# An order table in place of a list scheduler, in an attention and FFN kernel on one Trainium2 core

## The chip, the cores and the metric

The kernel runs on one core of a Trainium2 chip. The metric is the device time of one execution in microseconds; the program has one launch. The core has five engines with queues of their own: TensorE (PE in the profile; PEld is its weight load), VectorE (DVE), ScalarE (ACT), GpSimd (POOL) and SyncE (SP). Sixteen DMA engines move data for all of them.

## The reference

Windowed attention with sinks, then a gated feed-forward layer on its output, in float32:

```python
B, H, S, D = 4, 8, 768, 64;  n_sink, window = 4, 128
scores = q @ k.T / sqrt(D)                # per batch and head
keep = (key < n_sink) | (0 <= query - key < window)
a = softmax(where(keep, scores, -1e9))
x = (a @ v).transpose(0, 2, 1, 3).reshape(B * S, H * D)      # 3072 x 512
xn = x / sqrt(mean(x * x) + 1e-6) * rms_g
g = xn @ w_gate                           # 512 x 1536
out = (g * sigmoid(g) * (xn @ w_val)) @ w_out                # 1536 x 512
```

## The kernel before

**Blocks and groups.** The 3072 tokens are 24 blocks of 128, six for each of the four batches. Four blocks make a group of the feed-forward layer, six groups in all. A block g goes through these steps:

- q, k and v of the block are loaded. q and k of block 0 come through SP as float32 and are cast (`load_f32`, `cast`, L326 to L331). All others are loaded by POOL's software DMA, which casts to bf16 on the way (`load_bf16` L335, `load_v` L339). The gate and value weights come in tiles `w-a-b` (columns a to b of 12, `sw_w`, L381), the output weights in two tiles (`sw_wo`, L387).
- q and k are transposed: by TensorE and a copy for blocks 0 to 7 (`pe_t` L428, `copy_t` L435), by a DMA on SP's queue from block 8 on (`dma_t`, L442).
- Scores (`scores` L468, `scores_last` L484 for the last block of a batch), exp on ScalarE (L516, L492), masks. For blocks 0 and 1 a TensorE product adds the mask ahead of the scores (`mask_bias`, L450); up to block 15 VectorE multiplies by a mask (L533, L499); from 16 on POOL does it (L538, L505). From the third block of a batch on, four sink keys take part (`sink_k`, `sink_v`, `sink_s`, `sink_e`; L644 to L680).
- The attention product with v (`av`, L552 to L569), the division by the sum (`normal`, L580 and L581, tile x), the square on ScalarE (L589), the rms chain and the scaled xr on VectorE (`rms`, L596 to L613).
- xr is transposed into xnt, by TensorE and a copy for blocks 0 to 7 (`pe_x` L628, `copy_x` L634), by a DMA on SP's queue from block 8 on (`dma_x`, L640).

A group then takes chunks of the gate and value products, each into one PSUM bank (`mms`, L863, tiles g and v; in the profile v is also the name of the attention's v). A chunk is 4 weight columns by one block for group 0 (matmuls of 128 columns), 2 by two blocks for groups 1 and 2 (256), 1 by four blocks after that (512). Tanh is on ScalarE (L870), the two products that make hT are on VectorE (p L876, hT L886). The output product (L896, in three parts of four matmuls per block), its evacuation (L904) and the store by SP (L908) follow. The last block's output is cut into halves (L914 to L932).

**What sets the order.** The kernel does not issue instructions directly. Each step is an operation that is given to `Plan.op` with its engines and durations (`ways`), the tokens that it needs and gives, a priority, and the PSUM banks that it takes and drops. `Plan.run` (L70) then works through all of them as a list scheduler: among the operations whose needs are given it picks, again and again, the one that its own clock lets start first, by priority among equals. DMA landings are estimated by `Plan.land` (L50). The functions are called in that order, and each engine runs its instructions in it. So the order is fixed when the program is built; on the chip an engine waits only for data and buffers. The needs that stand for timing alone (such as `("s", g - LOAD_LEAD)` in `sw_block`, or `sw` n-8) are the planner's; on the chip POOL's load n waits for the landing of load n-8, as its DMA waits in the trace show.

The software loads' order is a string, in which `qkv-2` stands for three loads:

```python
LOADS = "q-1 k-1 v-0 w-0-2 v-1 qkv-2 qkv-3 w-2-4 w-4-6 w-6-8 w-8-9 w-9-10 w-10-12 qkv-4 wo-0-6 qkv-5 wo-6-12 qkv-6 qkv-8 qkv-7"
LOADS += "".join(f" qkv-{g}" for g in range(9, NB))
```

`WARM` = 30 products of zeros (L403) fill TensorE's waits at the start. The float32 product `unit_gb` (L411) spreads rms_g over the partitions.

Of the kernel before, what the change touches and what calls it, by code (L numbers as in the profile page):

```python
# [10 lines left out]
ACT = mybir.ActivationFunctionType  # L11
FP32 = mybir.dt.float32
BF16 = mybir.dt.bfloat16
I32 = mybir.dt.int32

P = 128
# [8 lines left out]


class Plan:

# [4 lines left out]
    LATE = 300  # L33
    RESERVE = 8
    HOP = {"PE": 40, "ACT": 35, "DVE": 35, "POOL": 90, "SP": 60}
# [7 lines left out]
    def op(self, ways, needs=(), gives=(), prio=0.0, takes=(), drops=(), ring=None, work=0.0,  # L43
           mode=0):
        self.ops.append(dict(
            ways=ways, needs=set(needs), gives=tuple(gives), prio=prio, takes=tuple(takes),
            drops=tuple(drops), ring=ring, work=work, mode=mode, at=len(self.ops), ready=0,
        ))
# [20 lines left out]

    def run(self):  # L70
        free, users = dict(self.START), {}
        self.loads = sum(o["ring"] == "POOL" for o in self.ops)
        wait = {o["at"]: set(o["needs"]) for o in self.ops}
        cand = {e: [] for e in free}
        left = len(self.ops)
        for o in self.ops:
            for t in o["needs"]:
                users.setdefault(t, []).append(o)
            if not o["needs"]:
                for e in o["ways"]:  # L80
                    cand[e].append(o)
        busy, warm, mode, order = [], False, 0, []
        while left:
            first = None

            many = min(
                (o for o in cand["PE"] if len(o["takes"]) > self.RESERVE), default=None,
                key=lambda o: o["prio"],
            )
            for e, found in cand.items():  # L90
                for o in found:
                    k = len(o["takes"])
                    if k > len(self.banks):
                        continue
                    ready = o["ready"] + self.HOP[e] if o["ready"] else 0
                    if k:
                        ready = max(ready, sorted(self.banks.values())[k - 1] + 40)
                    start = max(free[e], ready)
                    if (k and many and o["prio"] > many["prio"] and start > many["ready"]
                            and len(self.banks) - k < len(many["takes"])):  # L100
                        continue
                    key = (start, o["prio"], ready, o["at"])
                    if first is None or key < first[0]:
                        first = key, e, o
            if first is None:
                raise RuntimeError("stuck: %s" % [
                    (o["gives"], list(wait[o["at"]])) for o in self.ops if o["at"] in wait
                ][:20])
            (start, *_), e, o = first
            for x in o["ways"]:  # L110
                cand[x].remove(o)
            wait.pop(o["at"])
            left -= 1
            ns, lat, fn = o["ways"][e]
            if e == "PE":
                busy = [(a, d) for a, d in busy if a > start - 3413]
                warm = start - free[e] < 4000 and (warm or sum(d for a, d in busy) > 3000)
                ns = ns if warm else 2 * ns
                if o["mode"] != mode:
                    ns, mode = ns + 110, o["mode"]  # L120
                busy.append((start, ns if mode != 2 else 0))
                lat = ns + 180
            for s in o["takes"]:
                i = min(self.banks, key=lambda i: (self.banks[i], i))
                del self.banks[i]
                self.held[s] = i
            free[e] = start + ns
            end = start + lat
            if o["ring"] is not None:
                end = self.land(o["ring"], end, o["work"]) + self.LATE  # L130
            for s in o["drops"]:
                self.banks[self.held[s]] = end + 12
            for t in o["gives"]:
                for x in users.pop(t, ()):
                    x["ready"] = max(x["ready"], end + 12)
                    w = wait[x["at"]]
                    w.discard(t)
                    if not w:
                        for way in x["ways"]:
                            cand[way].append(x)  # L140
            order.append((start, end, e, fn, o))
        return order


@with_exitstack
def kernel(
# [13 lines left out]
    nc = tc.nc  # L160
# [15 lines left out]
    VW = D + 1  # L176
# [7 lines left out]
    POOL_AT = (1,2)  # L184
    DEPTH = 8
    LOADS = "q-1 k-1 v-0 w-0-2 v-1 qkv-2 qkv-3 w-2-4 w-4-6 w-6-8 w-8-9 w-9-10 w-10-12 qkv-4 wo-0-6 qkv-5 wo-6-12 qkv-6 qkv-8 qkv-7"
# [75 lines left out]
    dve(70, lambda: nc.vector.memset(ident, 0.0), gives=["id0"], prio=-99)  # L262
    dve(130, lambda: nc.vector.memset(bias.bitcast(I32), 0), gives=["bias0"], prio=-98)
    for b in range(B):
        dve(60, lambda b=b: nc.vector.memset(V16[b][:, :, :, D:VW], 1.0),
            gives=[("vone", b)], prio=-97 + b if b == 0 else -50)
# [47 lines left out]
    dve(130, other_bias, [("bias", 0)], [("bias", 1)], -60)  # L314
    dve(220, cut_ident, ["ident"], ["idnos"], -59)
    dve(700, make_masks, [("bias", 0), ("bias", 1)], ["masks"], MASKS_PRIO)
    dve(300, make_sel, ["ident"], ["sel", "headm"], MASKS_PRIO + 1)

# [41 lines left out]
    def sw_load(fn, gives, work, ns=870, needs=()):  # L360
        n = len(issue)
        more = [("sw", n - DEPTH)] if n >= DEPTH else []
        op({"POOL": (ns, 1900, fn)}, list(needs) + more, list(gives) + [("sw", n)], -89 + n,
           ring="POOL", work=work)
        issue.append(n)
# [35 lines left out]
    def warm(i):  # L401
        ps = bank(("warm",)) if i == 0 else BANK[("warm",)]
        nc.tensor.matmul(out=ps[:, 0:P], lhsT=zeros, rhs=zeros, start=True, stop=True)  # L403

    for i in range(WARM):
        pe(55, lambda i=i: warm(i), ["zeros"] + ([("warm", i - 1)] if i else []),
           [("warm", i)], 1e9, takes=[("warm",)] if i == 0 else (),
           drops=[("warm",)] if i == WARM - 1 else ())

# [5 lines left out]

    pe(1000, unit_gb, ["ones", "grow"], ["gbm"], GB_PRIO, takes=[("gb",)], mode=2)
    act(490, scale_gb, ["gbm", "table"], ["gb"], drops=[("gb",)])
# [157 lines left out]
    def normal(g, u):  # L575
        if u == 0:
            T["x16", g] = xpool.tile([P, H, D], BF16, name="x16")
        pvv = BANK.pop(("av", g, u))[:, 0:HW].rearrange("p (h c) -> p h c", c=VW)
        rden = small.tile([P, 4], FP32, name="rden")
        nc.vector.reciprocal(out=rden, in_=pvv[:, :, D])  # L580
        nc.vector.tensor_tensor(  # L581
            out=T["x16", g][:, 4 * u:4 * u + 4, :], in0=pvv[:, :, 0:D],
            in1=rden.unsqueeze(2).to_broadcast((P, 4, D)), op=ALU.mult,
        )
# [119 lines left out]
    def block_scores(g):  # L704
# [10 lines left out]
        for n0, n1 in parts:  # L715
            needs = [("kT", g)] + [("qT", g + i) for i in range(n0, n1)] + gate_of(g)
            needs += [("mb", g)] if g < PE_MASKS else []
            last = (n0, n1) == parts[-1]
# [19 lines left out]
            for u in range(2):  # L738
                for hi in range(2):
                    act(215 * (n1 - n0) + 55,  # L740
                        lambda g=g, u=u, hi=hi, n=(n0, n1), last=last: exps(g, u, hi, *n, last),
                        [("s", g, n0), "table"] + ([("av", g - 2, u)] if g >= 2 else [])
                        + ([("x", g, u, 0, n0)] if hi else []),
                        [("x", g, u, hi, n) for n in range(n0, n1)], early,
                        drops=[("s", g, u, hi)] if last else ())
# [16 lines left out]
    for g in range(NB):  # L762
# [21 lines left out]
        if t + 1 == NT:  # L784
            slots = [("s", g, hi) for hi in range(2)]
            needs = [("kT", g), ("qT", g)] + gate_of(g)
            if b in MERGE:
# [150 lines left out]
    def ffn(G, n, fts, cols, prio):  # L938
# [3 lines left out]
        keys.append(key)  # L942
        pe(864, lambda: mms(bank(("g", key)), wg, G, fts, cols),
           xs + [("wg", ft) for ft in fts], [("g", key)], prio, takes=[("g", key)])
        pe(864, lambda: mms(bank(("v", key)), wv, G, fts, cols),
           [("g", key)] + [("wv", ft) for ft in fts], [("u", key), ("F", G, n)], prio - 0.5,
# [39 lines left out]

    order = plan.run()
    with tc.manual_schedule():
# [36 lines left out]
```

## Time and profile before

| | |
|---|---|
| runs | 245.15, 245.25, 245.61 us; median 245.25 |
| profiled execution | span 243.9 us from the first instruction's start to the last one's end; the rest of a run's time lies around it |
| TensorE | busy 235.3 us (96%), 2116 matmuls |
| VectorE | busy 181.1 us (74%) |
| ScalarE | busy 131.2 us (54%) |
| POOL | busy 89.5 us (37%), 86 loads among it |
| DMA | 27.35 MB; the software queue moved 13.90 MB, SP's and ACT's 12.99 MB |

A row of the profile names engine, line, operation and tiles (output<-inputs). A row of TensorE with `x16` is sixteen matmuls in a row; the span of one includes its pipeline, so the distance of starts tells what one costs. Under "DMA to landing" stands the time from the issue of a DMA to the semaphore that tells of its landing. A wait in brackets names what came last. Positions of software loads are counted in POOL's order.

### The profile page before, as it was taken

The page shows a single profiled execution, that of the slowest core. Times are in us where ns is not written, and L with a number is a line of the kernel's source. Part 1 is how long each engine was busy: PE and PEld are TensorE (multiplying, and loading weights), DVE is VectorE, ACT ScalarE, POOL GpSimd, SP SyncE. Part 2 cuts the span into 40 slices and gives each one's busy share as a digit, 9 for nine tenths or more (in the row PEclk, how much of TensorE's full clock was granted, in tenths as well). Part 3 has the DMA queues.
Part 4 walks back from the last instruction along what each step waited for, and adds up shares of the span by engine and source line. Part 5 has one row for each costly group of instructions (what it writes and reads, how often), then busy time and mean ns, then how long its engine had stood idle before and what let it go on. Part 6 is the DMA issues. An engine that isn't in the chain of part 4 may idle for free.

```text
span 243.9 us, 5513 instructions
## 1 busy us (share of the span) xinstructions
PE 235.3 (96%) x2116; PEld 148.4 (61%) x2116; DVE 181.1 (74%) x481; ACT 131.2 (54%) x268; POOL 89.5 (37%) x116
## 2 busy tenths in 40 slices
PE   4988999999999999999999999999999999999994
PEld 2558987884788875587786544544554444444443
DVE  4279979896999999999899789896379760377700
ACT  4686565769684827584844574572553311333111
POOL 8976785596435546344520130321320000000000
PEclk9999999999999999999999999999999999999999
DMA  9999999999999999999999461110231002200022
GB/s 127 151 167 196 186 187 187 159 133 163 141 194 162 155 154 156 162 225 137 128 131 143 110 171 25 22 22 21 91 108 24 1 0 86 86 3 0 0 86 86
DMA packets 113579, 27.35 MB, mean 112 GB/s; under 512 B 103697, under 2 KB 110609, under 8 KB 113554
## 3 DMA queue, kind: packets, MB, share of 16 engines
q0 software_dynamic: 81760, 13.90, 80.6%
q1 hardware_dynamic: 31650, 12.99, 28.6%
q8 instruction: 16, 0.26, 0.4%
q10 hardware_dynamic: 144, 0.13, 0.2%
q14 instruction: 9, 0.07, 0.1%
HBM read 28.31 MB, written 6.29 MB: 142 GB/s over the span
## 4 chain that ended last, share of the span: by engine, by line
PE 76%; DMA 15%; DVE 4%; POOL 2%; issue 1%; POOLq 0%
PE v L863 23%; PE g L863 22%; PE o L896 20%; DMA wv<-in_moe_w_val_dram 7%; DMA q<-in_q_dram 5%; PE s L468 3%; DMA v<-in_v_dram 3%; PE av L569 2%; PE av L562 1%; PE av L552 1%; PE o_last L914 1%; DVE e L533 1%; DVE x L581 1%; POOL wg L381 1%; POOL wv L381 1%
## 5 line engine op out<-in xcount | busy, mean ns | idle before, releaser
L863 PE MATMUL v<-xnt,wv 128*128 128x128 bf16 (+2 forms) x528 | 71.1, 282 | 0.0
L863 PE MATMUL g<-xnt,wg 128*128 128x128 bf16 (+2 forms) x528 | 69.8, 282 | 0.3 <-DMA wg<-in_moe_w_gate_dram 0.2
L870 ACT ACTIVATE th<-g 128x512 bf16<-128x512 f32 x72 | 43.2, 600 | 50.0 <-PE g L863 47.4
L896 PE MATMUL o<-wo,hT 128*128 128x512 bf16 x276 | 65.4, 379 | 0.0
L876 DVE SCALAR_TENSOR_TENSOR p<-th,g 128x512 bf16<-128x512 bf16 x72 | 47.9, 682 | 21.6 <-ACT th L870 21.4
L863 PEld LDWEIGHTS <-wg 128*128 128x128 bf16 x528 | 43.1, 98 | 19.7 <-DMA wg<-in_moe_w_gate_dram 0.6
L863 PEld LDWEIGHTS <-wv 128*128 128x128 bf16 x528 | 43.1, 98 | 19.2 <-issue 0.5
L886 DVE TENSOR_TENSOR hT<-p,v 128x512 bf16<-128x512 bf16 x72 | 47.1, 680 | 1.5 <-PE v L863 0.7
L516 ACT ACTIVATE e<-s 128x512 bf16<-128x512 f32 (+1 forms) x88 | 43.8, 569 | 7.2 <-PE s L468 5.8
L896 PEld LDWEIGHTS <-hT 128*128 128x128 bf16 x276 | 25.3, 98 | 26.5 <-issue 1.5
L904 ACT ACTIVATE osb<-o 128x512 f32<-128x512 f32 x23 | 13.8, 601 | 23.4 <-PE o L896 23.4
L335 POOL DMA_DIRECT2D k<-in_k_dram x23 | 20.4, 886 | 16.3 <-DMA v<-in_v_dram 11.3
L339 POOL DMA_DIRECT2D v<-in_v_dram x24 | 21.3, 886 | 11.6 <-DMA q<-in_q_dram 10.5
L335 POOL DMA_DIRECT2D q<-in_q_dram x23 | 20.5, 891 | 11.7 <-DMA k<-in_k_dram 4.0
L581 DVE TENSOR_TENSOR x<-av,rden 128x256 bf16<-128x256 f32 x48 | 20.4, 424 | 1.7
L589 ACT ACTIVATE sq<-x 128x512 bf16<-128x512 bf16 x24 | 15.1, 630 | 11.4 <-DVE x L581 11.3
L613 DVE SCALAR_TENSOR_TENSOR xr<-x,r,gb 128x512 bf16<-128x512 bf16 x24 | 18.0, 751 | 0.9
L533 DVE TENSOR_TENSOR e<-e,masks 128x1024 bf16<-128x1024 bf16 x26 | 17.0, 684 | 1.4 <-ACT e L516 1.4
L538 POOL TENSOR_SCALAR_AFFINE_SELECT e<-e 128x512 bf16<-128x512 bf16 x10 | 6.4, 637 | 31.6 <-ACT e L516 16.1
L569 PE MATMUL av<-v,e 128*128 128x65 bf16 x192 | 17.1, 193 | 0.4 <-ACT e L516 0.3
L562 PE MATMUL av<-v,e 128*128 128x65 bf16 x160 | 15.1, 193 | 0.0
L569 PEld LDWEIGHTS <-e 128*128 128x128 bf16 x192 | 13.0, 97 | 3.3 <-ACT e L516 0.7
(75 smaller groups left out, 181.1 us busy)
## 6 DMA issues: line engine op xcount, KB each, us to landing
out_dram<-osb SPq DMA_DIRECT2D x23, 256.0 KB, 2.3
v<-in_v_dram POOLq DMA_DIRECT2D x24, 128.0 KB, 11.7
q<-in_q_dram POOLq DMA_DIRECT2D x23, 128.0 KB, 12.5
k<-in_k_dram POOLq DMA_DIRECT2D x23, 128.0 KB, 11.8
wo<-in_moe_w_out_dram POOLq DMA_DIRECT2D x2, 768.0 KB, 11.1
wg<-in_moe_w_gate_dram POOLq DMA_DIRECT2D x5, 256.0 KB, 7.7
wv<-in_moe_w_val_dram POOLq DMA_DIRECT2D x5, 256.0 KB, 8.1
stage<-in_k_dram SPq DMA_DIRECT2D x1, 256.0 KB, 3.3
```

What stands on the lines that cost most here:

```text
L335: nc.gpsimd.dma_start(out=T[name, g], in_=block_of(src, g))
L339: nc.gpsimd.dma_start(out=V16[b][:, t, :, 0:D], in_=block_of(v, g))
L516: nc.scalar.activation(out=T["e", g, u][:, 2 * hi:2 * hi + 2, n0:n1, :].rearrange("p x n c -> p x (n c)"), in_=ps.rearrange("p (j c) -> p ...
L533: nc.vector.tensor_tensor(out=ev, in0=ev, in1=mv, op=ALU.mult)
L569: nc.tensor.matmul(out=dest, lhsT=own, rhs=V16[b][:, t, h, :], start=(t == 0), stop=True, skip_group_check=True,)
L581: nc.vector.tensor_tensor(out=T["x16", g][:, 4 * u:4 * u + 4, :], in0=pvv[:, :, 0:D], in1=rden.unsqueeze(2).to_broadcast((P, 4, D)), op=AL ...
L613: nc.vector.scalar_tensor_tensor(out=T["xr", g], in0=T.pop(("x16", g)).rearrange("p h d -> p (h d)"), scalar=r[:, 3:4], in1=gb, op0=ALU.mu ...
L863: nc.tensor.matmul(out=ps[:, i * n:(i + 1) * n], lhsT=w_sb[:, kt, ft * P:(ft + 1) * P], rhs=T["xnt", G][:, kt, cols], start=(kt == 0), sto ...
L870: nc.scalar.activation(out=T["th", key], in_=BANK[("g", key)], func=ACT.Tanh, scale=0.5,)
L876: nc.vector.scalar_tensor_tensor(out=T["p1", key], in0=T.pop(("th", key)), scalar=1.0, in1=BANK.pop(("g", key)), op0=ALU.add, op1=ALU.mult,)
L886: nc.vector.tensor_tensor(out=T[hk][:, i:i + n, cols], in0=T.pop(("p1", key)).rearrange("p (n c) -> p n c", n=n), in1=BANK.pop(("v", key)) ...
L896: nc.tensor.matmul(out=BANK[("o", G, tb)], lhsT=T["h", G, ft // 4][:, ft % 4, tb * P:(tb + 1) * P], rhs=wo[:, ft, :], start=(ft == 0), sto ...
```

## The change

`Plan.run` no longer chooses. It takes `ORDER`, a table with the numbers of the operations for each engine, and at each step only works out which engine's next operation starts first by its clock; this decides in what sequence the functions are called, and which PSUM bank a product gets. An operation's number is its place among the calls of `Plan.op`, which is the same in both kernels.

- POOL's table begins: v of block 0; the mask bias; q, k of 1; the identity; gate tile 2-4; q of 2; v of 1; q of 3; k of 2; k of 3; gate tile 0-2; value tiles 0-2 and 2-4; v of 2; gate tiles 4-6 and 6-8; value tiles 4-6 and 6-8; gate tiles 10-12, 8-9 and 9-10; value tiles 8-9, 9-10 and 10-12; q, k of 4; q, k of 5; v of 3; the first output tile; k of 6; v of 5; q of 6; v of 4; q of 8; the second output tile; k of 7; q of 9; q of 7. Later loads are not in the order of blocks either: v of 19, 21, 23 stand at places 52, 66 and 76 of 86, v of 13, 15, 14 and 16 at 73, 80, 81 and 84.
- SP's table begins with rms_g, then q and k of block 0 (before: k, q, rms_g). Its transpositions and stores are in another order.
- TensorE's table begins with eight of the zero products, then the product for gb, the mask product of block 0, and k 0, q 0, q 1, k 1; the same products stand ahead of the first weight chunk as before. The first gate chunk of group 2 now stands ahead of ten products that were ahead of it (columns 10 and 11 of group 1, attention of blocks 12 and 13, outputs of two blocks of group 1, one sink product).
- Seven copies and casts change between VectorE and ScalarE.
- Durations in some calls are new (they only serve the planner's clock), as are some needs that fix an order of scores and exps; the zero products no longer share one bank.

```diff
+def span(text):
+    ids = []
+    for x in text.split():
+        a, _, b = x.partition("-")
+        ids += range(int(a), int(b or a) + 1)
+    return ids
...
-    def run(self):
-        free, users = dict(self.START), {}
+    def run(self, table):
+        ids = {e: span(table[e]) for e in self.START}
+        free, at, users, last = dict(self.START), dict.fromkeys(self.START, 0), {}, []
...
-            for e, found in cand.items():
-                for o in found:
...
-                    key = (start, o["prio"], ready, o["at"])
-                    if first is None or key < first[0]:
-                        first = key, e, o
+            for e in self.START:
+                if at[e] == len(ids[e]):
+                    continue
+                o = self.ops[ids[e][at[e]]]
+                k = len(o["takes"])
+                if wait[o["at"]] or k > len(self.banks):
+                    continue
...
+                if o["ring"] == "POOL" and len(last) >= self.DEPTH:
+                    ready = max(ready, last[-self.DEPTH])
+                start = max(free[e], ready)
+                if first is None or start < first[0]:
+                    first = start, e, o
...
+ORDER = {
+    "PE": """
+114 115 122 125 127 132 113 130 136 142 140 138 170 172 143 148 174 162 155 175 118 153
...
+    "POOL": """
+22 9 20 21 8 32 26 25 29 27 30 23 24 33 28 34 36 35 37 42 38 40 39 41 43-45 48 49 31 47
+53 50 52 46 55 51 59 61 58 62 63 56 57 54 71 64 83 60 67 65 68 73 93 66 77 79 74 70 69
+76 72 82 87 97 85 90 99 100 104 95 88 91 80 75 96 98 105 94 86 92 81 78 89 102 453 84
...
+    "SP": """
+18 16 14 314 330 315 346 331 347 654 649 362 377 664 363 398 329 376 415 399 414 345 659
...
     def warm(i):
-        ps = bank(("warm",)) if i == 0 else BANK[("warm",)]
+        ps = bank(("warm", i))
...
             needs = [("kT", g)] + [("qT", g + i) for i in range(n0, n1)] + gate_of(g)
+            needs += [("s", g - 1)] if g and not merged else []
...
-    order = plan.run()
+    order = plan.run(ORDER)
```

## The prediction

> **What bounds the kernel now.** I read the page first, then TensorE by stage, then the chain of waits by place, then the landings of DMAs, because an order table can only move waits.
>
> The page's slices:
> ```profile
> PE   4988999999999999999999999999999999999994
> DVE  4279979896999999999899789896379760377700
> DMA  9999999999999999999999461110231002200022
> ```
> TensorE is full from the fourth slice (18 us) to the end. The DMA engines are full for 22 slices (134 us): until then a transfer moved ahead pushes others back. VectorE is nearly full from 60 to 110 us.
>
> The stages (columns: stretch, its length, busy us of PE, weight loads, DVE, ACT, POOL, clock, DMA, GB/s):
> ```profile
> 15.00:20.00 5.00, 3.78 (x61) 2.69 (x60) 4.54 (x21) 4.26 (x13) 4.20 (x6) 1.00 1.75 185
> 20.00:25.00 5.00, 4.80 (x92) 4.60 (x89) 4.62 (x11) 3.21 (x8) 2.97 (x4) 1.00 1.49 193
> 60.00:80.00 20.00, 20.00 (x212) 15.80 (x210) 19.18 (x52) 14.04 (x31) 9.01 (x11) 1.00 1.87 171
> ```
> So any gain is a lead won before about 33 us, plus the small waits after it. TensorE's timeline has the points that I count from:
> ```profile
> 19.69 1.06 PE L863 MATMUL g<-xnt,wg 128*128 128x128 bf16 x16
> 32.62 1.06 PE L863 MATMUL v<-xnt,wv 128*128 128x128 bf16 x16
> 52.07 0.39 PE L428 MATMUL q<-ident,q 128*128 128x128 bf16 x4
> 80.33 0.27 PE L552 MATMUL av<-vsk,esk 128*128 128x260 bf16 x1
> 102.67 1.58 PE L863 MATMUL g<-xnt,wg 128*128 128x256 bf16 x13
> 240.57 0.42 DVE L925 TENSOR_SCALAR last<-o_last 128x256 f32<-128x256 f32 x1 [9.61 <-PE o_last L914]
> ```
> They are: the first weight product; the value product of columns 8 to 11 of block 0, which ends the weight loading; the transposition of q of block 7; block 9's first attention product; the first gate product of group 2 (it reads the transposed x of blocks 8 and 9); the end of the last product. Matmuls of 512, 256 and 128 columns start 216, 109 and 56 ns apart there. The waits that are left after 33 us are 0.24 us at 46 us (q of block 6) and 0.17 us at 102.25.
>
> Landings, DMA to landing as min/median/max; the transposed x (L640) from 76 to 101 us, the same after 135 us, then a load of v (L339) issued at 41.36:
> ```profile
> L640 SPq DMA_TRANSPOSE xnt<-xr x4: 1224/1269/1582, 78.8 to 100.5; - x4
> DMA to landing us min/median/max: 7.1/7.5/8.4
> DMA to landing us min/median/max: 2.4/2.4/2.9
> DMA to landing us min/median/max: 9.6/9.6/9.6
> ```
> A DMA transposition needs 7 us or more while software loads are queued, and 2.4 us when they are over.
>
> The profiled span is 243.87 us, the runs' median 245.25: 1.38 us lie around the span. I sum against the span and add 1.38.
>
> **The change, part by part.** *The same work.* Each engine's instructions are the same in kind but for seven copies that change between ScalarE and VectorE, and TensorE enters or leaves the 64-row form once more (a score product behind a 512-column one costs 312 for 216 ns): 0.1 us. The new costs in the planner (memsets, masks, chunks of 896) issue nothing. The added needs only fix an order that the table already has.
>
> *The start.* v of block 0 is issued before q and k of block 1. Landings before were q 1.32+5.0 = 6.3, k 2.66+4.4 = 7.1, v 3.82+6.1 = 9.9: the third load lost some 2 us. The third is now k of block 1, and its transposition stands ahead of the first scores, so they start near 9.9+0.1+0.4 = 10.4 instead of 9.24 (L468). If the delay belonged to v alone, k lands near 8.7. Against that, the fp32 product for gb (L411, 2.07 us at half clock) leaves the path between the q transpositions and the scores, and q of block 3 comes as the seventh software load, not the tenth, so the scores of block 2 no longer hold the first weight product (0.48 us at 18.74). The first weight product should stand near 18.7 (17.6 to 19.7), where 19.69 was.
>
> *The weights.* All tiles are loaded after the same loads but one: v of block 3 (1.0 us) goes behind them. The last value tile landed at 32.57 and should land at 31.5. The work ahead of the 32.62 point is the same in both orders, so the lead there is 1.0 us, at most 1.5.
>
> *The lead is lost at q of block 7.* It becomes the 38th software load. The 38th landed at 41.36+9.6 = 50.9. Of the first 38, two v are now q or k (1.0 and 0.85 apart in landing): -0.3. But q of block 8 now comes five loads earlier, and its DMA transposition starts ahead of q of block 7: from 53.7 to 116.4 us 35 loads landed, which undisturbed need 31.9 of the 62.7 us; 26 transpositions and 8 stores took the rest, 0.9 us each. So q of block 7 lands at 50.9-0.3+0.9 = 51.5. The order before it holds a 512-column output part (0.86) in place of a value chunk and a transposition (0.89+0.22), 0.25 us less. Before, that point stood at 52.07-0.25 = 51.8. **Lead: 0.3 us** (1.5 if the third load lost nothing, as all later landings come 1.2 earlier; 0 at the other end). What comes earlier than this at the start is only a longer wait here; without this wait the lead would be the 1.0 above.
>
> *A new wait at group 2.* The table calls the first gate product of group 2 much earlier: ten products (columns 10 and 11 of group 1, outputs of two blocks, attention of blocks 12 and 13) now stand behind it. Between block 9's first attention product and it TensorE has: five attention products 1.77, four chunks 3.49, eight output parts 6.91, scores of blocks 11 to 13 with their form changes 1.67, two small ones 0.25, together 14.1 us; before it was 22.3 (102.67-80.33). In that time x of block 9 must come through VectorE and the DMA transposition. VectorE's new order puts, after that product (0.35 and 0.25 handover): x, hT, a mask, a memset, x, p (3.05 us), then x of block 10 (waits for TensorE until 3.95; to 4.5), p behind the square and the tanh on ScalarE (to 5.6), x (6.15), two last masks (6.9), p (7.5), then the rms chain of block 9 (1.76, as from 85.20 to 86.96): 9.25, issue at 9.35. Plus 7.1 us to land, the least in the row, as it stands alone in SP's queue: 16.45, and 0.05 to TensorE. **The wait is 16.5-14.1 = 2.4 us**. With 8.4 us to land it is 3.7; with 2.4 it is nothing. I take 7.1, as the software loads still run in that stretch (the DMA row is full to 134 us). Queued behind on TensorE is everything, so the whole wait counts; VectorE and ScalarE catch up meanwhile, so I expect the 0.17 us at 102.25 to go, and a like amount of small waits.
>
> The Trainium skill (DMA: Bandwidth & Descriptors, Anatomy of one DMA) gives a DMA as about 2.0 us plus bytes over 436 GB/s, an estimate of 2.3 us for such a 128 KB transposition. The trace has 2.4 after 135 us and 7.1 to 8.4 under loads; by the page's rule there would be no wait at group 2, and the sum would be a gain of 0.5.
>
> *The late loads.* The table pulls some loads far ahead (v of blocks 19, 21, 23) and leaves v of blocks 13 to 16 and k of 15, 17, 18 to places 72 to 84. The loads' total is the same and they always queue, so a late place is a late landing: the 81st was issued at 111.72 and landed at 122.55. In the new order some four transpositions and three stores fewer come before it (7 x 0.9), so v of block 14, now the 81st, lands near 116.3. Its product stands 20.6 us of TensorE work behind group 2's first, which starts near 99.5 (80.33+3.0 for what the new order puts ahead, -0.3, +16.5): near 120, covered by 3.8 us. v of block 16 is issued only after a mask on POOL; about even. Bounds 0 to 2 us; I take 0, as the nearer row covers it.
>
> *The sum.* -0.3 (lead) -0.3 (small waits) +2.4 +0.1 (form change) = +1.9 us: span 245.7, time 247.1. The tail (last products, evacuations, stores: 240.57 to 243.87) holds the same steps.
>
> **The rivals.** *A, the forecast:* slower by 1.9, by the wait at group 2. For: 7.1 to 8.4 for every transposed x in that stretch. Against: VectorE's chain is counted by hand. Chance 0.58.
> *B, the start holds:* the third load loses nothing, lead 1.5. Then +0.7, and with 6.8 to land (the least of q and k from 60 to 100 us) +0.4: 245.7 to 246. For: v before had no other reason to be late. Against: it landed late by its place. Chance 0.16, most of it slower by over 0.2% (0.5 us, about what a measurement here can tell), the rest within.
> *C, faster:* SP's transposition of x of block 9 lands before TensorE gets there. It decides at 14.1-9.35 = 4.7 us from issue to landing; below that there is no wait, and the lead and the small waits stay: -0.5 to -1.7, so 243.5 to 244.7. For: the 2.4 us without load. Against: none under 6.8 while loads run. Chance 0.14.
> *D, the late loads bite:* v of blocks 13 to 16 land behind their products, +2 to +4 more, 249 to 251. For: each waits on a saturated queue; against: the 3.8 us above. Chance 0.12.
> That the table does not do what it says is excluded: the instructions as built stand in its order.
>
> **How the numbers follow.** A gives 247.1. The range takes its bounds. Above: no lead, and 8.4 us to land: +0.3+1.3, 248.7, and 0.2 of D's edge: 248.9. Below: B's +0.4 with VectorE's chain at 8.5 (without its wait for the tanh, 0.8 less): -0.4, 244.9. Left out are C and most of D, some 0.2. Faster by over 0.2%: C, 0.14. Within: B's lower half and A's lowest edge, 0.13. Slower: 0.73, A, D and the rest of B.
>
> The Trainium skill (TensorE: Matmul & The Clock Gate, Part 1) says that the full clock comes after about 3.4 us of sustained work; here work ran from 4.16 us and the 512-column matmuls still started 403 to 427 ns apart, with 216 only from 11.4. An earlier full clock would shorten the start, which the wait for q of block 7 swallows.
>
> **What would show it.** Right: the first weight product near 18.7, TensorE's wait for a DMA of q near 51.5, and one of about 2.4 us before L863 near 99 to 100, with xnt's transposition issued some 7 us before. Wrong: no idle time there (then C), a first weight product near 17.5 with q of block 7 near 50.3 (B), or waits of av for v past 105 us (D).

## The result and the profile after

| | before | changed |
|---|---|---|
| runs | 244.59 to 246.18, median 245.22 us | 254.04, 257.45, 257.97, 258.96, 259.19, 259.86 us, median 258.47 |
| profiled execution | span 243.9 | span 252.3 (its run: 254.04 us, the shortest of the six) |

The changed kernel is slower by 13.3 us in the median, where 1.9 was forecast. The ratio, 1.043 (95% interval 1.037 to 1.049), is taken from the two shortest runs alone (254.04 and 257.45), and by these two the kernel is 10.5 us slower.

The slices of the changed kernel's page, in the order of those shown of before, and with the clock:
```profile
PE   6899999809999999799999999999999999999994
PEclk9999999967999999999999999999999999999999
DVE  2488888419899989988889889986379986335450
DMA  9999999999958999999979224612001520000214
```
TensorE fills up earlier than before (a 9 from the third slice on, where before had it from the fifth). Then there is what before did not have: a slice with no TensorE work (from 50 us), VectorE nearly empty in the same place, a granted clock of 0.6 and 0.7 in it and behind it, and a hole in the DMA row (slices 12 and 13, from 69 us), where it was full to 134 us before. The second thin place of TensorE, near 103 us, is the wait that was forecast.

The stages, as shown of before (stretch, length, busy us of PE, weight loads, DVE, ACT, POOL, clock, DMA, GB/s):
```profile
15.00:20.00 5.00, 4.70 (x81) 3.88 (x77) 4.61 (x18) 4.95 (x14) 3.48 (x5) 1.00 1.63 190
20.00:25.00 5.00, 4.98 (x91) 4.63 (x90) 3.97 (x14) 2.88 (x6) 3.11 (x4) 1.00 1.48 198
60.00:80.00 20.00, 19.89 (x212) 14.49 (x212) 18.16 (x53) 14.97 (x32) 2.83 (x4) 1.00 1.01 112
```
The start is denser (4.70 and 4.98 us of TensorE where before had 3.78 and 4.80), while from 60 to 80 us POOL has 4 instructions where before had 11, and the DMA share falls from 1.87 to 1.01.

TensorE's and VectorE's timelines at the first hole (start, duration, engine, line; in brackets the idle time ahead and what ended it):
```profile
48.75 1.03 PE L952 MATMUL o<-wo,hT 128*128 128x512 bf16 x4
56.41 0.58 PE L481 MATMUL q<-ident,q 128*128 128x128 bf16 x4 [6.64 <-DVE hT L942]
```
```profile
46.29 0.68 DVE L932 SCALAR_TENSOR_TENSOR p<-th,g 128x512 bf16<-128x512 bf16 x1
55.64 0.72 DVE L942 TENSOR_TENSOR hT<-p,v 128x512 bf16<-128x512 bf16 x1 [8.68 <-DMA v<-in_v_dram]
55.75 0.10 DVE L320 MEMSET v<- 128x48 bf16 x1
```
TensorE waits 6.64 us for a PSUM bank that hT (the second of the two products behind a chunk) has to read out. VectorE had nothing to do with a load of v by its arithmetic; but ahead of that hT stands a memset of 0.1 us, operation 3, which sets the column of ones behind each head's 64 columns of v, for the whole of batch 1. It writes the tile into which the loads of v of blocks 6 to 11 go. In the order of the calls it stands behind the loads of v of blocks 9, 8 and 6, and in the built program it waits for the landing of all three (52.9, 54.6 and 55.5). A semaphore wait on the memset's own line, the longer of two, shows it:
```profile
L320 DVEq EVENT_SEMAPHORE  x2: 21/1316/2611, 52.9 to 92.7; - x2
```
It begins at 52.9 and takes 2.61 us, up to the last landing. (The table has the memset ahead of that hT. In the rows the two start 0.11 us apart, and the profile puts the idle time on hT's row.) Before, the four memsets were among the first eight instructions of VectorE.

The same tile holds up the loads behind the memset. POOL's timeline, and TensorE's waits by total (waiter, what it waited for, us, times, longest):
```profile
59.60 0.91 POOL L390 DMA_DIRECT2D q<-in_q_dram  x1
77.68 1.76 POOL L394 DMA_DIRECT2D v<-in_v_dram  x2 [17.17 <-DVE v L320]
```
```profile
PE q L481 <- DVE hT L942: 6.6, 1, 6.6
PE g L919 <- DMA xnt<-xr: 1.6, 1, 1.6
```
v of block 19, pulled far ahead by the table, waits 17.17 us for the memset of batch 3, and all loads behind it in the queue with it: that is the hole in the DMA row. v of block 7 waited 3.68 us for the memset of batch 1. The second line of waits is group 2; the transposed x of block 9 was issued at 99.13 and landed at 105.50:
```profile
105.64 0.60 PE L919 MATMUL g<-xnt,wg 128*128 128x256 bf16 x4 [1.65 <-DMA xnt<-xr]
```

The clock, in TensorE's windows of the same stretch (stretch, length, busy us, granted clock, DMA share, GB/s):
```profile
44.00:50.00 6.00, 5.72 (x85) 1.00 1.94 169
50.00:52.50 2.50, 0.00 (x0) 1.00 2.60 152
52.50:56.50 4.00, 0.09 (x2) 0.54 2.91 136
56.50:59.50 3.00, 3.00 (x18) 0.50 1.96 133
59.50:62.00 2.50, 2.45 (x38) 0.98 1.88 97
```
Some 3 us into the wait the clock is halved, and it stays so for 3 us after work resumes.

### The profile page after: what moved, and what is told of

It is laid out like the page before. It is cut to its first block, busy times and chain, and to the rows that moved or that the text cites. A ratio compares the mean times of both kernels' runs of the same rounds, so it can differ in the third digit from the quotient of the medians.

```text
span 252.3 us, 5420 instructions
## 1 busy us (share of the span) xinstructions
PE 235.0 (93%) x2093; PEld 148.7 (59%) x2116; DVE 184.1 (73%) x482; ACT 126.7 (50%) x267; POOL 90.1 (36%) x116
## 4 chain that ended last, share of the span: by engine, by line
PE 59%; DMA 17%; POOL 12%; DVE 7%; issue 3%; ACT 0%; POOLq 0%; DVEq 0%
PE o L952 18%; PE v L919 17%; PE g L919 17%; DMA v<-in_v_dram 6%; DMA wo<-in_moe_w_out_dram 5%; DMA wg<-in_moe_w_gate_dram 4%; POOL v L394 3%; POOL q L390 3%; DMA xnt<-xr 3%; POOL k L390 2%; PE s L521 2%; DVE p L932 2%; DVE hT L942 1%; POOL wv L435 1%; PE av L622 1%
## 5 line engine op out<-in xcount | busy, mean ns | idle before, releaser
L919 PE MATMUL g<-xnt,wg 128*128 128x128 bf16 (+2 forms) x526 | 70.9, 282 | 2.0 <-DMA xnt<-xr 1.6
L919 PE MATMUL v<-xnt,wv 128*128 128x128 bf16 (+2 forms) x524 | 71.9, 282 | 0.2
L952 PE MATMUL o<-wo,hT 128*128 128x512 bf16 x259 | 66.8, 383 | 1.1 <-issue 0.2
L942 DVE TENSOR_TENSOR hT<-p,v 128x512 bf16<-128x512 bf16 x72 | 47.7, 683 | 26.0 <-PE v L919 16.2
L926 ACT ACTIVATE th<-g 128x512 bf16<-128x512 f32 x72 | 40.7, 603 | 40.7 <-PE g L919 40.6
L932 DVE SCALAR_TENSOR_TENSOR p<-th,g 128x512 bf16<-128x512 bf16 x72 | 47.7, 680 | 13.5 <-ACT th L926 13.3
L919 PEld LDWEIGHTS <-wv 128*128 128x128 bf16 x528 | 43.8, 99 | 20.7 <-issue 0.8
L569 ACT ACTIVATE e<-s 128x512 bf16<-128x512 f32 (+1 forms) x88 | 44.2, 573 | 10.6 <-PE s L521 9.3
L666 DVE SCALAR_TENSOR_TENSOR xr<-x,r,gb 128x512 bf16<-128x512 bf16 x24 | 19.0, 793 | 0.9
L622 PE MATMUL av<-v,e 128*128 128x65 bf16 x192 | 16.7, 193 | 0.1
L615 PE MATMUL av<-v,e 128*128 128x65 bf16 x160 | 14.8, 193 | 0.0
```

The source lines that it names most:

```text
L569: nc.scalar.activation(out=T["e", g, u][:, 2 * hi:2 * hi + 2, n0:n1, :].rearrange("p x n c -> p x (n c)"), in_=ps.rearrange("p (j c) -> p ...
L622: nc.tensor.matmul(out=dest, lhsT=own, rhs=V16[b][:, t, h, :], start=(t == 0), stop=True, skip_group_check=True,)
L666: nc.vector.scalar_tensor_tensor(out=T["xr", g], in0=T.pop(("x16", g)).rearrange("p h d -> p (h d)"), scalar=r[:, 3:4], in1=gb, op0=ALU.mu ...
L919: nc.tensor.matmul(out=ps[:, i * n:(i + 1) * n], lhsT=w_sb[:, kt, ft * P:(ft + 1) * P], rhs=T["xnt", G][:, kt, cols], start=(kt == 0), sto ...
L926: nc.scalar.activation(out=T["th", key], in_=BANK[("g", key)], func=ACT.Tanh, scale=0.5,)
L932: nc.vector.scalar_tensor_tensor(out=T["p1", key], in0=T.pop(("th", key)), scalar=1.0, in1=BANK.pop(("g", key)), op0=ALU.add, op1=ALU.mult,)
```

## The experiments

Theory M: the late memsets, by waiting for loads into their own tile, cost everything beyond the forecast. Rivals: the late q of block 7 and other late loads set the time (Q); the hold of the load queue is what costs, not VectorE's wait (H); the place of the instructions in VectorE's order, and not the wait (P).

**e1: all memsets first.** VectorE's table:
```diff
-1 2 6 7 10 0 11 15 12 139 13 173 163 ... 245 633 3 634 ... 290 679 5 322 ... 340 704 354 4 342
+1 2 6 7 10 0 11 15 12 139 13 3 4 5 173 163 ... 245 633 634 ... 290 679 322 ... 340 704 354 342
```


> The changed kernel with one edit: the memsets of the ones column of v's tiles for batches 1, 3 and 2 (operations 3, 5, 4; L320) go back to the start of VectorE's table. Theory M (memsets): in the table they stand behind loads of v into the same tile, so VectorE waits for those loads (8.68 us, longest wait before 55.64), TensorE goes without hT for 6.64 us and its clock falls; the loads of v behind them wait in turn (17.2 us at v of block 19). Without that: no VectorE wait at 47 us, no gap in the software loads at 67 to 77 us, granted clock full throughout, a wait of about 1.1 us for q of block 7 near 50.5 and of about 2 us for the transposed x at group 2 near 98; span 243.8, time 245.2 (244.4 to 246.5), within 0.5% of before. Rival Q (late q): q of block 7, loaded as the 38th and landing at 50.9, and the other late loads set the time anyway: TensorE still waits over 4 us near 50, time 252 or more.

Measured: 247.18 us (246.22 to 247.77, 6 runs), ratio 1.007 (1.0047 to 1.0094). Q falls: 11.3 us go with the place of three instructions of 0.1 us (8.6 us counted from the two runs of the ratio). The clock is 1.0 in the profile. M's number was 2 us too low, and its list of waits was right in part. Two rows of TensorE's timeline:
```profile
52.19 0.40 PE L481 MATMUL q<-ident,q 128*128 128x128 bf16 x4 [1.26 <-DMA q<-in_q_dram]
91.08 0.61 PE L521 MATMUL s<-qkT 64*128 64x256 bf16 x8 [1.41 <-DVE y L653]
```
The wait for q of block 7 is there (1.1 expected). The 2 us at group 2 are not; in their place the scores of block 12 wait 1.41 us. The engine named there is not the one: the DMA transposition of q of block 12 was issued at 82.17 and landed at 90.99, just ahead of 91.08.

**e2 and e3: one part of the memsets first.** e2 moves operation 3 alone (as in e1), e3 operations 5 and 4 alone.

> Only the memset of batch 1 goes to the start of VectorE's table; those of batches 3 and 2 stay late. Theory M: the 6.6 us wait and the fall of the clock go, the hold of v of block 19 behind the memset of batch 3 stays (some 10 us in which no software load is issued), and makes the scores of block 12 wait some 1.7 us: time 247.0 (246 to 248.5), clock full. Rival H (the hold of the loads is what costs): time stays above 250.

> Only the memsets of batches 2 and 3 go to the start; that of batch 1 stays late. Theory M: TensorE's wait of 6.6 us near 50 and the half clock after it stay, the gap in the loads at 67 to 77 us goes: span near 250.5, time 252 to 257 (with the same spread as the changed kernel has, if the spread comes from the clock), granted clock near 0.98. Rival H: 247 or less.

Measured: e2 254.56 us in the median, with 250.11, 254.35, 254.77 and 255.11; e3 256.33 (255.61 to 257.58), clock 0.973 to 0.986. e3 lies in M's range, though its span (253.9) is 3.4 us above the one expected: the memset of batch 1 alone costs 9.1 us over e1. e2 missed M's range in all four runs and lies where rival H has it. The hold of the loads alone costs 2.9 us in the one run with the clock at 1.0, and 7.2 to 7.9 in the three others (clock 0.986 or 0.987). Its profile, of one of those, shows how; the first row is of POOL, the others of TensorE:
```profile
POOL v L394 <- DVE v L320: 15.4, 1, 15.4
53.95 0.61 PE L481 MATMUL q<-ident,q 128*128 128x128 bf16 x4 [2.88 <-DMA q<-in_q_dram]
105.38 1.87 PE L919 MATMUL g<-xnt,wg 128*128 128x256 bf16 x8 [3.22 <-DMA xnt<-xr]
```
The wait for q of block 7, 1.26 us in e1, is 2.88 here, one of 3.22 stands at group 2, where e1 has none, and behind each the clock falls to 0.5. So H holds for a part. What the hold adds to a late memset of batch 1 is not shown: e3, which is without it (255.61 to 257.58), takes as long as the changed kernel, which has both (254.04 to 259.86). In e2's trace q of block 7 was issued 0.6 us later than in e1's and took 12.3 us or more to land, where e1's took 11.1 to 11.5; why was not found.

**e4: the fault put into the kernel before.**
```diff
     order = plan.run()
+    at = [x[4]["at"] for x in order]
+    late = order.pop(at.index(3))
+    at.remove(3)
+    order.insert(at.index(262), late)
```


> The kernel before with one edit: the memset of batch 1's ones column is issued late, just ahead of the rms factor of block 4 (operation 262), behind the loads of v of blocks 6 to 9 in program order. Theory M: VectorE waits there until v of block 9 lands (near 58), TensorE idles 6 to 9 us and its clock falls: span 251 to 256, time 253 to 258, clock below 0.99. Rival Q: the kernel before has no late q of block 7, so it moves by less than 2 us: 245 to 247.

Measured: 254.00 us (252.94 to 254.81), ratio 1.035 (1.032 to 1.038), clock 0.986. VectorE waits 6.3 us for v, TensorE 5.4:
```profile
DVE rden L580 <- DMA v<-in_v_dram: 6.3, 1, 6.3
PE x L628 <- DVE x L581: 5.4, 1, 5.4
```
One late memset costs the old order 8.7 us, much as it does the new (9.1).

**e9: the wait taken out, the place kept.** The table is the changed kernel's; the late operations write ones elsewhere.
```diff
+    scratch = const.tile([P, NT * H], BF16, name="scratch")
+
+    def ones_of_v(b):
+        if b:
+            nc.vector.memset(scratch, 1.0)
+        else:
+            for i in range(B):
+                nc.vector.memset(V16[i][:, :, :, D:VW], 1.0)
+
     for b in range(B):
-        dve(140, lambda b=b: nc.vector.memset(V16[b][:, :, :, D:VW], 1.0),
+        dve(140, lambda b=b: ones_of_v(b),
```


> The changed kernel with its table untouched; the three late memset operations (3, 5, 4) stay where the table has them but write ones to a scratch tile of the same 128x48 elements, and the first one (operation 2) sets the ones columns of all four batches, three short instructions more at the start. Theory M, in full: it is the wait for the loads into the same tile that costs, not the place or the work of the late instructions: no VectorE wait near 47 us, no hold of the loads, the time of e1, 247.2 (246.2 to 248). Rival P (the place in VectorE's order, which shifts what stands behind): time 253 or more.

Measured: 247.21 us (246.18 to 249.6, 10 runs), ratio 1.0088 (1.0053 to 1.0123). P falls: the same instructions in the same places cost nothing once they do not touch v's tiles. TensorE's wait for q of block 7 and the one at group 2 in its timeline:
```profile
51.49 0.40 PE L490 MATMUL q<-ident,q 128*128 128x128 bf16 x4 [1.11 <-DMA q<-in_q_dram]
98.28 2.78 PE L928 MATMUL g<-xnt,wg 128*128 128x256 bf16 x24 [0.94 <-DMA xnt<-xr]
```

Its trace has the changed kernel's order but for the waits, so the two can be set against each other point by point (start in us; the last column is what the point lost between the two):

| TensorE's point | before | changed | e9 | changed - e9 |
|---|---|---|---|---|
| first weight product | 19.69 | 17.79 | 17.86 | -0.1 |
| value columns 8 to 11, block 0 | 32.62 | 30.32 | 30.43 | -0.1 |
| transposition of q of block 7 | 52.07 | 56.41 | 51.49 | 4.9 |
| scores of block 6 | 55.46 | 60.26 | 53.80 | 6.5 |
| scores of block 12 | 90.99 | 95.40 | 88.98 | 6.4 |
| first gate product of group 2 | 102.67 | 105.64 | 98.28 | 7.4 |
| last matmul | 240.26 | 248.70 | 241.34 | 7.4 |

4.9 us are the longer wait, 1.5 the half clock behind it, 0.9 come between the scores of block 12 and group 2, most of it the longer wait there (1.65 against 0.9), and that is the whole span's difference (252.3 - 244.9 = 7.4). What the other runs of the changed kernel lost beyond that (up to 5.8 us, at a mean clock of 0.978 to 0.980 instead of 0.986) has no trace. An estimate: 0.980 over a span of 256.3 us is 10.2 us at half clock, where the profiled run had 6.8; 3.4 us more at half clock cost at most 1.7 of the 4.0 us between the two, so the rest should be longer waits.

**e5: the wait filled.** 28 products that are thrown away stand in the place of the idle time.
```diff
         n = cols.stop - cols.start
+        if w_sb is wg and G == 0 and fts[0] == 8 and cols.start == 3 * P:
+            for _ in range(28):
+                nc.tensor.matmul(out=ps, lhsT=zeros, rhs=wo[:, 0, :], start=True, stop=True)
```


> The changed kernel, memsets left late, with 28 products of zeros by 512 columns (28 x 216 ns = 6.0 us) written into the bank of the gate product of block 3, columns 8 to 11, ahead of its own products (mms, L915), just before TensorE's long wait near 50 us. They add 6 us of TensorE work that is thrown away, in the place of idle time. Theory G (the clock falls because TensorE idles for 3 us or more, and that is a price of its own): the granted clock stays full, the span is about 1.5 us under that of the changed kernel (252.3), time 251.5 to 253, and the runs lie closer together than 254.0 to 259.9. Rival S (the clock falls for another reason, or its fall costs nothing): time 254 to 260 as without the products, or longer by what they add.

Measured: 257.33 us (255.33 to 257.8). As a forecast of the time this failed. TensorE's windows, of the stretch behind the filled wait and of that around group 2:
```profile
56.50:59.50 3.00, 2.59 (x29) 1.00 2.10 134
102.00:110.00 8.00, 5.21 (x34) 0.79 2.05 156
```
Where it was to act it did: the clock is full where the changed kernel had 0.50, and from q of block 7 to the scores of block 6 it takes 2.65 us instead of 3.85. But the first weight product came at 19.11 in this run instead of 17.79, the wait at group 2 grew to 2.8 us, and there the clock fell. The later start is no work of the edit, which acts from 48 us on: the same four products of 512 columns take 1.04 us in the changed kernel (first row) and 1.89 here (second), as the full clock had not come yet.
```profile
10.02 1.04 PE L503 MATMUL s<-bias,ident 128*128 128x512 bf16 x4
10.72 1.89 PE L503 MATMUL s<-bias,ident 128*128 128x512 bf16 x4
```
The price of a fall is shown at its place, 1.2 to 1.5 us; that saving it saves time in the end is not. The run with a mean clock of 0.998, which is 1.0 us at half clock, took 255.33 us all the same.

**e6 and e7: is the forecast's wait at group 2 there?** e6 is e1 with q of block 12 earlier, e7 is e6 with xr of block 9 earlier.
```diff
 POOL  -... 68 73 93 66 77 79 74 70 69      +... 68 73 70 93 66 77 79 74 69
 SP    -... 363 398 329 376 415             +... 363 398 376 329 415
 DVE   -723 356 713 358 366 368 718 344 714 +723 356 344 713 358 366 368 718 714   (e7 only)
```


> e1 with q of block 12 loaded five places earlier (ahead of v of block 19 in POOL's table) and its transposition ahead of that of x of block 8 in SP's. Theory W (the lead is spent on the transposed x of block 9 for group 2, as the prediction put it; the 1.5 us wait of the scores of block 12 in e1 only took its place): that wait goes, a wait of 1.5 to 3 us comes up before the first gate product of group 2 near 98, and the time is e1's within 0.5 us: 247.2 (246.2 to 247.9). Rival L (a late load, q of block 12, is what costs): no new wait, time 245.2 to 246.

> e6 with the rms chain and xr of block 9 (operation 344) six operations earlier in VectorE's table, about 4 us, so that the transposition of x of block 9 starts earlier. Theory W: the wait at group 2 shrinks by what xr comes earlier, less what the delayed operations cost (a wait of about 1.2 us near 89 for the work that VectorE now does later): 245.4 to 246.6, about 1 us under e6. Rival L: no change against e6 within 0.4 us.

Measured: e6 246.76 and 247.22 us at a clock of 1.0, 251.26 and 254.42 in two runs at 0.985 or 0.986. The scores of block 12 start with no wait, and group 2 has one, in TensorE's timeline:
```profile
98.36 0.81 PE L919 MATMUL g<-xnt,wg 128*128 128x256 bf16 x6 [1.08 <-DMA xnt<-xr]
```
W holds by the two runs at full clock: taking away one wait brings up the other, and the time stays e1's. e7 missed its number: 247.47 (246.24 to 248.2 in four runs, one of 251.13). The wait at group 2 is gone, but the scores of block 12 wait 0.56 us, and the output part behind them 0.18, for the VectorE work that was put behind xr, and the span is 244.8 where e6 had 245.1. Putting 4 us of VectorE's work behind xr gave the gain back in the same stretch.

**e10: the load order alone, with the list scheduler.**
```diff
-LOADS = "q-1 k-1 v-0 w-0-2 v-1 qkv-2 qkv-3 w-2-4 ..."
+LOADS = "v-0 q-1 k-1 q-2 v-1 q-3 k-2 k-3 w-0-2 w-2-4 v-2 w-4-6 w-6-8 w-8-9 w-9-10 w-10-12 qk-4 qk-5 v-3 wo-0-6 ..."
-load_v(g), [("v", g)], 910, needs=needs)
+load_v(g), [("v", g)], 910, needs=needs + [("vone", g // NT)])
```


> The kernel before, its list scheduler kept; only LOADS is set to the changed kernel's order up to block 8 (v of block 0, q and k of 1, q of 2, v of 1, q of 3, k of 2 and 3, then the weights, v of 3 behind them, and so on; a gate tile and its value tile together), and a load of v needs the memset of its tile, so that no memset can stand behind a load. What the load order alone brings when the scheduler fits the rest to it. Theory W (the early loads win 1 to 2 us at the first weight product, and later landings take it back): first weight product near 18.6, the value product of columns 8 to 11 of block 0 near 31.7, time 245 to 247.5. Rival E (the early loads are a gain in themselves, which the changed table gives away): time below 244.7.

Measured: 248.14 us (247.22 to 248.69), ratio 1.012 (1.008 to 1.017). It lies outside W's range (245 to 247.5). Rival E falls, and so does W's lead: the first weight product starts at 19.43, the 32.62 point at 32.42. These early loads alone win 0.2 us at the weights. They are not quite the changed kernel's: with the added need the scheduler issues q of block 1 ahead of v of block 0, and the first gate tile is the ninth load, not the fourth. So the lead of 2 us in the changed kernel is not shown to be that of its loads; the other engines' orders may be needed for it. The added need matters: without it the scheduler puts the first memset behind the load of v of block 0. Where the time behind the weights goes (2 us at the last matmul) was not traced.

**e8: an order searched for.** e1's tables with 307 operations moved a few places, as a diff counts them (TensorE 93, VectorE 71, POOL 56, ScalarE 47, SP 40). Some of the places (q_1 is q of block 1, wg_2 the gate tile from column 2, g and u the gate and value chunks by group, column and token):
```diff
 POOL (tiles)  -v_0 bias q_1 k_1 ident wg_2 q_2 v_1 q_3 k_2 k_3 wg_0 ... q_8 wo_6 k_7 q_9 q_7
               +bias q_1 ident k_1 k_3 v_1 v_0 q_2 k_2 q_3 wg_0 wv_0 ... wo_6 q_8 q_7 k_7 v_6 q_9
 PE (chunks)   -... g_2_0_0 g_2_2_0 g_2_4_0 u_1_10_256 u_2_0_0 u_2_2_0 ...
               +... u_1_10_256 ... g_2_6_0 g_2_2_0 g_2_4_0 u_2_2_0 u_2_4_0 g_2_0_0 u_2_0_0 ...
```


> e1's tables with some 300 of the 1066 operations moved by a few places, chosen so that none of the waits found so far should be left: q of block 7 loaded before k of block 7, q and k of block 1 and k of block 3 ahead of v of block 0, the first gate product of group 2 behind three other products of group 2 that do not stand so early, xr of block 9 earlier. The estimate from the durations of the traces is 3 us under e1: span 242 to 243, time 243.5 to 244.5, and so below the kernel before (245.2), with the first weight product near 17.9 and no wait over 0.7 us after 33 us. If the lead at the weights (1.2 us in e1) cannot be kept past 50 us by any order, because the landings of q set it, the time is 245 or more.

Measured: 244.08 us (243.76 to 245.64, 12 runs), ratio 0.996 (0.994 to 0.998): 0.4% faster than the kernel before, and within the 243.5 to 244.5 that were expected. TensorE's slices, and the two largest of its waits in total, behind that for the first product (the first of the two is at 10.6 us):
```profile
PE   7899999999999999999999999999999999999994
```
```profile
PE vs L707 <- DMA v<-in_v_dram: 0.9, 1, 0.9
PE v L920 <- DMA wv<-in_moe_w_val_dram: 0.4, 2, 0.2
```
No wait over 0.24 us is left behind 33 us. Its lead is 2.6 us at the first weight product, 2.0 at the 32.62 point and 1.8 at the last matmul (238.44 against 240.26).

## Why the prediction was wrong, step by step

**The step that failed** is in its list of VectorE's new order: "x, hT, a mask, a memset, x". That memset is operation 4, the ones of batch 2. It was priced as work, 0.1 us, and the question what it waits for, and who waits for it, was not asked; nor were operations 3 and 5 looked for in the rest of the list, though the table had moved all three from VectorE's first instructions deep into its list: 3 and 4 behind loads of v into their own tile, 5 ahead of a load of v (block 19) that then waits for it. "The new costs ... issue nothing" and "the same in kind" were true and beside the point: an instruction of the same kind in another place has other waits. Operation 4 itself cost 0.69 us of VectorE; of the two that were not listed, operation 3 cost VectorE 8.68 us and operation 5 held the loads for 17.17 us. Without these waits the kernel takes 247.2 us (e1, e9), with them 258.5 in the median. The needs written in the kernel do not have this wait. It exists only in the built program, because one instruction writes column 64 of a tile whose columns 0 to 63 the loads write: no byte is shared, but the tile is.

**No rival named it.** D had the nearest price (249 to 251), by late loads; no wait of an attention product for v shows in the changed kernel. All four cases shared the same list of waits, so the range was wide in the sizes of known terms and had nothing for one that was left out.

**The other steps** can be read in e9 and e1, where the memsets do not wait:
- The start: the third load was said to lose 2 us. It was issued at 3.85 and landed at 9.09, 5.2 us, where v had taken 6.1 and k, in second place, 4.4: it lost 0.8 us at most, which is near to B's condition. The first weight product stood at 17.8, not 18.7. In the eight traces whose loads begin like this it stood between 17.7 and 19.1, so one trace tells a lead at the start to 1 us or so.
- The lead at the weights: 1.0, at most 1.5, was forecast; 2.3 in the changed kernel, 2.2 in e9, 1.2 in e1. Too small in the first two, by the start above; right in e1.
- The lead lost at q of block 7: 0.3 was forecast. It is 0.58 in e9 (with a wait of 1.11 us for q) and -0.12 in e1 (1.26). Right: whatever the start won beyond that became wait.
- The wait at group 2: 2.4 was forecast, near 99 to 100; 1.65 in the changed kernel, 1.08 in e6, 0.9 in e9, nothing in e1, where the scores of block 12 had taken 1.41 of it. Right in place and cause, too long by 0.7 to 1.5: in the changed kernel the transposition took 6.37 us to land (99.13 to 105.50), not 7.1. In e9, counted from block 9's first attention product (82.98), it was issued after 8.85 us (9.35 forecast) and took 6.3, and TensorE got there after 14.4 (14.1). The formula of the Trainium skill that the prediction set beside its rows (DMA: Bandwidth & Descriptors, Anatomy of one DMA) is given there for DMAs that GpSimd issues; these are SP's.
- The late loads at nothing: right for v. But q of block 12, now the 57th load and not the 51st, was transposed so late in e1 that its scores waited 1.41 us; no term of the prediction has that.
- The sum of these, +1.9: e1 is 1.9 us above before (247.18 against 245.26), e9 2.0 (247.21 against 245.18). The sum is that of the changed kernel without its memsets. That it fits to 0.1 us is partly luck: a larger lead and a smaller wait than forecast, both lost in small waits, cancel.
- Three readings were off, without weight in the sum: TensorE's row has an 8 in the fourth slice and 9 from the fifth (24 us); q of block 8 comes two places earlier (34 for 36), not five; at the start products of 512 columns came 216 ns apart only from 12.2 us, not 11.4.

## What to carry to other kernels

When an order is changed, look at every instruction that moved for what it waits for as built, not for what it takes: a memset of 98 ns behind loads into its own tile cost 9 us, and the same memset on another tile nothing. Fill constant columns before the first load into their tile is issued, or give them a tile of their own, and write that as a need wherever an order is chosen by program. A lead won early is worth only what the next landing lets through: here 2 us at the weights were 0.6 at q of block 7, and it took other orders of loads and products all the way (e8) to keep 1.8.

## What the runs showed of the hardware

**The clock falls within a wait.** Waits of 1.08 to 1.65 us left the granted clock at 1.00; waits of 2.8 (e5), 2.88, 3.22 (e2), 5.4 (e4), 6.64 and 7.3 us (e3) were followed by the half clock. In these traces it fell 2.3 (e5) to 5.0 us (e3) after the last product and came back 2.8 to 5.4 us after work resumed. The Trainium skill (TensorE: Matmul & The Clock Gate, Part 1) has the array go to half clock after one idle window of about 3.4 us and asks for no gaps longer than that. The runs agree in kind, but a wait of 2.8 us was enough here.

**It moves in steps.** The half clock lasted 6.83 us in the changed kernel (52.80 to 59.62), e3 (55.48 to 62.31) and e4 (56.29 to 63.12), and 3.41 in both places of e2 (53.53 to 56.94, 104.73 to 108.14) and in e5 (106.68 to 110.10); between e2's two falls lie 51.2 us, 15 times 3.41. So the clock looks to be set anew every 3.41 us (worked out from these traces alone). Of the 3.41 us ahead of each fall TensorE was idle for 2.3 us or more; the wait of 1.65 us did not bring one. Where a wait falls against the steps then matters too.

**So a wait has a step in its price.** Behind the 6.64 us wait the half clock took 1.2 (against e5) to 1.5 us (against e9) more. Kernels with waits on this path can spread: e6 has runs of 247 us at a clock of 1.0 and of 251 and 254 at 0.986 and 0.985. In e2's trace the waits themselves are longer too; why they vary from run to run stays open.

**A DMA transposition is slow while software loads are queued.** In e1, with software loads queued, transpositions of q and k for blocks 12 to 14 took 8.0 to 9.0 us from issue to landing; three that were issued from 118.8 to 121.4, as the last load before a pause of the queue landed (119.8), took 2.4 to 2.5. The changed kernel shows the same within 20 us. Two transpositions that were issued at 57.5 and 58.8, with loads under way, took 6.8 and 7.6 us (first two rows; the row shown is of the second); three that were issued in the hold, in which POOL issued no load (60.5 to 77.7), took 2.4 (last two rows; of the two of k and one of q, the row of k is shown):
```profile
L495 SPq DMA_TRANSPOSE qkT<-k x1: 1281/1281/1281, 58.8 to 58.8; - x1
DMA to landing us min/median/max: 6.8/7.2/7.6
L495 SPq DMA_TRANSPOSE qkT<-k x2: 1188/1211/1234, 70.1 to 73.7; - x2
DMA to landing us min/median/max: 2.4/2.4/2.4
```
So with 2.5 us to land in place of 8.8 (an estimate from these rows) e1 would not have its wait at the scores of block 12.
